# A GFNet and GEGLU kernel on one core: norm 0 earlier, four tiles per bank for slabs 0 and 1, first loads in one queue

## The chip, the cores and the metric

The kernel runs on one core of a Trainium2 chip. The metric is device time in microseconds (us), lower is better. Engines are named as in the profile: PE (TensorE matmul), PEld (its weight load), DVE (VectorE), ACT (ScalarE), POOL (GpSimd) and SP (SyncE, here only a queue of transfers).

## The reference

The input `x` is 2048 x 640 in bf16. It is normalised along its 640 columns to `xn`. Two branches read `xn`; the result is `x + s * g`.

```python
xn = layernorm(x)                                   # (x - mean) / sqrt(var + 1e-5)
X  = rfft2(xn) * (w_r + 1j * w_i)                   # 2048 x 321 spectrum
s  = irfft2(X)                                      # 2048 x 640
g  = silu((gelu_tanh(xn @ w_gate) * (xn @ w_up)) @ w_down)   # 640 -> 1536 -> 640
return x + s * g
```

## The kernel before

**Data.** The 2048 rows stand as 16 slabs of 128 rows; slab `n1` holds rows `16*n2 + n1`. `X` is the whole input on chip, 16 x 640 elements on each of 128 partitions, and is normalised in place. A group is four slabs. `xnT[g]` holds the transposed normalised slabs of group `g`, 640 rows (five chunks of 128) by 512 columns: it is the moving operand of the up and gate products. `Wg`, `Wu` and `Wd` are the weights; the 1536 hidden columns are 12 tiles of 128. `UT` holds the product of gate and up of one group, transposed.

**The feed-forward stage.** For one tile and one `k` (0 gate, 1 up), `ffn_piece` issues five matmuls that add up in a PSUM bank `psg` or `psu`, of which there are two each. Then ACT applies GELU to the gate bank and writes `ge` (L837), and DVE multiplies the up bank with `ge` into `UT` (L839). A bank is free again when its reader is done.

**Order.** Everything is issued in an order written out by hand. PE runs through the list `back`; after entry `s` of `back` the items that were `put` at slot `s` are issued. Each engine runs its own instructions in that order. Entries 0 to 15 are the first part of group 0: entry 0 is slab 0 against tiles 0 and 1 (128 columns), with the transposes of slab 1 in its middle; entry 1 is slab 1 against the same tiles; entries 2 to 7 are tiles 2 to 7 against slabs 0 and 1 (256 columns), 8 to 15 are tiles 0 to 7 against slabs 2 and 3. From entry 16 on a tile and `k` have an entry each with 512 columns; slot 24 begins the down projection of group 0. The Fourier stages (`slab_S1`, `slab_D`, `s2_step` and so on) are put between later entries.

**Before entry 0.** `warm_pe(21)` issues 21 matmuls of 256 columns on ones, so that PE is running while the first loads arrive. On DVE stand `stats(0)` (two `bn_stats` of 320 columns each and their `bn_aggr`) and both halves of slab 1's statistics. `root_act(0)` has ACT make 1/sqrt(var + eps) of slab 0, and then load the GELU table; `root` of slab 1 takes the way over DVE (`ve`) and POOL (`pow`). `norm_parts(0)` normalises columns 0 to 383 and then 384 to 639; `slab_Tparts(0)` transposes the five chunks on PE and evicts them in two parts, the first by DVE, the second by ACT.

**Loads.** SP's queue brings the slabs, `Wu` tiles 0 to 5 and all that follows; ACT's queue brings `Wg` tiles 0 to 5, two tiles at a time. At most eight transfers are outstanding: the ninth waits for the first to land.

**POOL's part.** Besides the roots, POOL makes integer tables by `iota`, then six one-column constants in `inv_rest` (from five that DVE makes in `inv_consts`), the phases `tinv_phase` (two halves of 128 x 1024), `ft_phase(0, k)` in three steps, and then, put at slot 13, `root(4, 4)` and `shift(4, 4)`, which give scale and bias (`rst`, `nmr`) for `norm_act` of slabs 4 to 7 on ACT, put at slots 15, 17, 19 and 21.

Of the kernel before, what the change touches and what calls it, by code (L numbers as in the profile page):

```python
# [76 lines left out]
def build(nc, env):  # L77
# [5 lines left out]
    def load_x(n0, n, eng=nc.sync):  # L83
        eng.dma_start(out=X[:, n0:n0 + n, :], in_=xv[:, n0:n0 + n, :])

    def load_w(k, t0, t1, eng=nc.sync):
        f0, f1 = t0 * P, t1 * P
        eng.dma_start(out=(Wg, Wu)[k][:, :, f0:f1], in_=(wgv, wuv)[k][:, :, f0:f1])

    def load_gu(t0, t1):  # L90
        for k in range(2):
            load_w(k, t0, t1)

    load_x(0, 1)
    load_x(1, 1)
    load_w(1, 0, 2)
    load_w(1, 2, 4)
    load_x(2, 1)
    load_w(1, 4, 6)
    load_x(3, 1)  # L100
    load_gu(6, 8)
    load_x(4, 4)
    load_gu(8, 12)
    load_x(8, 4)
# [68 lines left out]
    def c1(name, dt=FP32):  # L173
        return consts.tile([P, 1], dt, name=name)
# [35 lines left out]
            rstd[n0 + k] = r[:, k:k + 1]  # L210

    def root_act(n1):
        rstd[n1] = c1("rst0")
        nc.scalar.activation(out=rstd[n1], in_=mva[n1 // 4][:, n1 % 4, 1:2], func=ACT.Abs_reciprocal_sqrt, bias=eps)
        nc.scalar.activation(out=warm, in_=negpi, func=ACT.Gelu_apprx_tanh)

    def norm(n1, c0=0, c1_=D):
# [10 lines left out]
    eps = c1("eps")  # L228
    nc.vector.memset(eps, 1e-5)
    nc.scalar.activation(out=warm, in_=eps, func=ACT.Abs_reciprocal_sqrt)  # L230
    for t in (0, 2, 4):
        load_w(0, t, t + 2, nc.scalar)
    b_0, b_1 = c1("b_0"), c1("b_1")
    nc.vector.memset(b_0, 320.0)
    nc.vector.memset(b_1, 0.0)
# [583 lines left out]
    def bank(k):  # L819
        return psA.tile([P, 512], FP32, tag="gu"[k], name="ps" + "gu"[k])  # L820
# [17 lines left out]
        else:  # L838
            nc.vector.tensor_tensor(out=UT[:, t, c0:c1_], in0=ps, in1=ges[t], op=ALU.mult)  # L839

    def ffn_part(g, t, h):
        for k in range(2):
            ffn_piece(g, t, k, h * 256, h * 256 + 256)

    def ffn_half(g, t, k):
        ffn_piece(g, t, k, 0, 512)
# [122 lines left out]
            if t == NT - 1:  # L969
                gated(g, j, k, ph)  # L970

    def ffn_slab(j, tk):
        for t, k in tk:
            ffn_piece(0, t, k, j * P, j * P + P)

    GG, UU = ((0, 0), (1, 0)), ((0, 1), (1, 1))

    def run(*items):
        for it in items:
            it[0](*it[1:])  # L980
# [3 lines left out]
    def norm_parts(n1):  # L984
        for a, b in PARTS:
            norm(n1, a * P, b * P)

    def slab_Tparts(n1):
        if n1 == 0:
            xnT[0] = slot(0, 5, 512)  # L990
        for (a, b), ev in zip(PARTS, (nc.vector.tensor_copy, nc.scalar.copy)):
            pt = psB.tile([P, 5, P], BF16, tag="b")
            for c in range(a, b):
                nc.tensor.transpose(out=pt[:, c, :], in_=X[:, n1, c * P:(c + 1) * P], identity=ident)  # L994
            ev(out=xnT[0][:, a:b, n1 * P:n1 * P + P], in_=pt[:, a:b, :])
        done.add(("T", n1))

    NP = 8
    STR = (1, 2)
    back = [(run, (ffn_slab, 0, GG), (norm_parts, 1), (slab_Tparts, 1), (vt_iota, 1), (ffn_slab, 0, UU),  # L1000
             (inv_consts, 0), (inv_consts, 1)),
            (run, (ffn_slab, 1, GG + UU), (stats, 2), (root, 2, 1))]
    for h in range(2):
        for t in range(0 if h else 2, NP):
            back.append((ffn_part, 0, t, h))
        if h == 0:
            back[-1] = (run, (ffn_piece, 0, NP - 1, 0, 0, 256), (slab_Tparts, 3), (ffn_piece, 0, NP - 1, 1, 0, 256))
    for g in range(4):
        for t in range(NP if g == 0 else 0, NT):
            for k in range(2):  # L1010
# [10 lines left out]
    def put(s, *item):  # L1021
        plan[s].append(item)

    put(1, inv_rest)
    put(2, norm, 2)
    put(3, bn_half, 3, 0)
    put(4, bn_half, 3, 1)
    put(4, bn_join, 3)
    put(4, root, 3, 1)
    put(4, slab_T, 2, 1)  # L1030
    put(5, norm, 3)
    for g in range(5):
        put(3 + g, ft_v, g)
        put(8 + g, ft_v, 5 + g)
# [98 lines left out]
        for k in range(n):  # L1133
            put(min(d + 8 + k, LAST), finish, n0 + k)

    warm_pe(21)
    bn_half(1, 1)
    bn_join(1)
    root(1, 1)
    norm_parts(0)  # L1140
    slab_Tparts(0)
    warm_pe(2)

    put(5, phase_const)

# [35 lines left out]
```

## Time and profile before

| | us |
|---|---|
| median of 3 runs | 193.73 (193.61 to 193.73) |
| the profiled execution | 193.65 |
| its span, first to last instruction | 191.9 |
| outside the span | 1.75 |
| PE busy | 186.1 |
| DVE busy | 150.9 |
| ACT busy | 131.9 |
| POOL busy | 53.9 |
| first warming matmul starts | 1.18 |
| first matmul of the feed-forward stage starts | 6.84 |
| entry 8 of `back` starts on PE | 16.50 |
| entry 16 of `back` starts on PE | 25.24 |

Times in the timeline are counted from the first instruction. A row of the timeline gives start, length, engine, line, operation, output and input, count, and in brackets how long the engine had been idle and what ended that. Matmuls overlap: a row of five that shows 0.71 us is followed by the next row after 0.55. The share of a queue entry named "SPq" or "ACTq" is the issue of a transfer, not the transfer.

### The profile page before, as it was taken

How to read it: one execution, taken by the hardware profiler on the slowest of the kernel's cores; microseconds unless marked ns; L12 is line 12 of the kernel's file. 1: busy time of each engine (PE TensorE's matmuls, PEld its weight loads, DVE VectorE, ACT ScalarE, POOL GpSimd, SP SyncE). 2: the span in 40 equal slices, each digit the busy share in tenths (PEclk: the TensorE clock that was granted, in tenths of full speed). 3: DMA queues.
4: the chain of work that ended last, by engine and by line, in shares of the span. 5: the costliest groups of instructions: out<-in, count | busy, mean ns of one | idle time of the engine just before them, and what ended most of it. 6: DMA issues, size and time to landing. Idle time of an engine off the chain costs nothing.

```text
span 191.9 us, 4068 instructions
## 1 busy us (share of the span) xinstructions
PE 186.1 (97%) x1453; PEld 115.6 (60%) x1469; DVE 150.9 (79%) x364; ACT 131.9 (69%) x241; POOL 53.9 (28%) x91
## 2 busy tenths in 40 slices
PE   7999999999999999999999999999999999999993
PEld 5788854677655665566543334347775555556772
DVE  6787889899799889846978677685445898888973
ACT  4658557957878778536697878634989776876622
POOL 4458768999040200000000000002030134150400
PEclk9999999999999999999999999999999999999999
DMA  6999999948889994249996444149900084778842
GB/s 164 300 329 360 370 332 170 172 99 318 178 165 191 211 300 120 78 111 230 223 108 123 106 103 103 42 107 273 266 5 0 0 117 111 152 153 213 121 174 62
DMA packets 39700, 32.43 MB, mean 169 GB/s; under 512 B 12928, under 2 KB 37760, under 8 KB 39552
## 3 DMA queue, kind: packets, MB, share of 16 engines
q1 hardware_dynamic: 35888, 27.91, 58.6%
q0 software_dynamic: 1824, 3.28, 9.4%
q10 hardware_dynamic: 1968, 0.98, 1.9%
q8 instruction: 11, 0.18, 0.4%
q14 instruction: 9, 0.07, 0.1%
HBM read 19.03 MB, written 7.88 MB: 140 GB/s over the span
## 4 chain that ended last, share of the span: by engine, by line
PE 95%; DMA 2%; DVE 1%; issue 1%; SPq 0%; ACT 0%
PE psu L832 27%; PE psg L832 27%; PE psg L967 7%; PE psg L933 7%; PE psu L967 6%; PE psu L933 5%; PE pu L657 2%; PE pd L762 2%; PE pv L735 2%; PE pz L555 2%; PE pd L573 2%; PE px L628 2%; DMA X<-in_A_x_dram 2%; PE pt L994 1%; PE pd L575 1%
## 5 line engine op out<-in xcount | busy, mean ns | idle before, releaser
L832 PE MATMUL psu<-XG,Wu 128*128 128x512 bf16 (+2 forms) x284 | 60.4, 342 | 0.5 <-issue 0.3
L832 PE MATMUL psg<-XG,Wg 128*128 128x512 bf16 (+2 forms) x280 | 60.1, 341 | 0.6
L839 DVE TENSOR_TENSOR UT<-psu,ge 128x512 bf16<-128x512 f32 (+2 forms) x58 | 34.4, 594 | 13.6 <-PE psu L832 8.1
L837 ACT ACTIVATE ge<-psg 128x512 bf16<-128x512 f32 (+2 forms) x58 | 30.3, 523 | 21.3 <-PE psg L832 20.6
L832 PEld LDWEIGHTS <-Wu 128*128 128x128 bf16 x290 | 25.9, 98 | 20.9 <-issue 3.4
L832 PEld LDWEIGHTS <-Wg 128*128 128x128 bf16 x290 | 26.5, 98 | 18.8 <-issue 0.2
L967 PEld LDWEIGHTS <-UT 128*128 128x128 bf16 x204 | 19.1, 98 | 6.9
L813 POOL DMA_DIRECT2D VY<-in_A_x_dram x12 | 10.6, 964 | 26.2 <-ACT W L737 10.5
L713 POOL COPY vr<-VY 128x128 bf16<-128x128 bf16 x2 | 0.6, 291 | 60.2 <-DMA VY<-UDR 60.2
L644 DVE TENSOR_TENSOR RZ<-xs,W 128x960 bf16<-128x960 bf16 (+2 forms) x22 | 13.3, 647 | 4.4 <-ACT xs L640 4.4
L967 PE MATMUL psg<-Wd,UT 128*128 128x320 bf16 (+1 forms) x108 | 15.7, 290 | 0.0
L578 ACT CAST RZ<-pd 128x660 bf16<-128x660 f32 x16 | 11.3, 706 | 5.2 <-PE pd L575 5.2
L189 DVE BATCH_NORM_STATS2 st<-X 128x6 f32<-128x320 bf16 x32 | 14.0, 476 | 0.6 <-DMA X<-in_A_x_dram 0.4
L933 PEld LDWEIGHTS <-UT 128*128 128x128 bf16 x120 | 11.4, 98 | 4.8 <-issue 0.4
L967 PE MATMUL psu<-Wd,UT 128*128 128x320 bf16 (+1 forms) x96 | 13.9, 293 | 0.0
L737 ACT CAST W<-pv 128x640 bf16<-128x640 f32 x16 | 11.1, 691 | 3.1 <-PE pv L735 3.1
L763 ACT ACTIVATE W<-pd 128x640 bf16<-128x640 f32 x16 | 11.3, 706 | 1.5 <-PE pd L762 1.5
L557 ACT CAST GEN<-pz 128x640 bf16<-128x640 f32 x16 | 11.2, 698 | 1.2 <-PE pz L555 1.2
L672 ACT CAST RX<-pu 128x480 bf16<-128x480 f32 (+3 forms) x22 | 10.8, 489 | 1.1 <-DVE RX L672 0.3
L640 ACT CAST xs<-px 128x960 bf16<-128x960 f32 (+2 forms) x11 | 10.3, 933 | 0.0
L207 POOL TENSOR_TENSOR rst<-ve,mhalf 128x1 f32<-128x1 f32 (+1 forms) x6 | 5.5, 913 | 11.5 <-DVE ve L205 11.5
L933 PE MATMUL psg<-X,UT 128*128 128x320 bf16 x48 | 7.8, 300 | 0.0
(202 smaller groups left out, 302.1 us busy)
## 6 DMA issues: line engine op xcount, KB each, us to landing
ZDR<-RZ SPq DMA_DIRECT2D x16, 160.5 KB, 4.1
UDR<-RX SPq DMA_DIRECT2D x10, 240.8 KB, 3.1
B<-ZDR SPq DMA_DIRECT2D x8, 240.8 KB, 5.2
W<-UDR SPq DMA_DIRECT2D x2, 963.0 KB, 9.1
X<-in_A_x_dram SPq DMA_DIRECT2D x3, 640.0 KB, 10.3
Wd<-in_B_w_down_dram SPq DMA_DIRECT2D x1, 1920.0 KB, 14.6
VY<-in_A_x_dram POOLq DMA_DIRECT2D x12, 160.0 KB, 4.3
out_dram<-VY SPq DMA_DIRECT2D x12, 160.0 KB, 2.8
```

Source lines behind the costliest of these rows:

```text
L189: nc.vector.bn_stats(out=st_n[n1][:, k, :], in_=X[:, n1, 320 * k:320 * k + 320])
L557: nc.scalar.copy(out=Zt[n1], in_=pz)
L578: nc.scalar.copy(out=zd.rearrange("p c (q e) -> p c q e", e=10), in_=pd[:, :, 0:330].rearrange("p c (e q) -> p c q e", q=33))
L644: nc.vector.tensor_tensor(out=pp[-1], in0=xs, in1=WT[:, :, h0:h0 + n, l0:l0 + w], op=ALU.mult)
L672: copy(out=out, in_=src)
L737: nc.scalar.copy(out=vs, in_=pv)
L763: nc.scalar.activation(out=parts(eobuf, i, 5)[:, :, n1 - DG[i][0], :], in_=pd, func=ACT.Copy, scale=(2.0 if n1 // 4 in BY_SILU else 1.0) / ...
L832: nc.tensor.matmul(ps, lhsT=WT[:, c, t * P:(t + 1) * P], rhs=xnT[g][:, c, c0:c1_], start=(c == 0), stop=(c == 4))
L837: nc.scalar.activation(out=ges[t], in_=ps, func=ACT.Gelu_apprx_tanh)
L839: nc.vector.tensor_tensor(out=UT[:, t, c0:c1_], in0=ps, in1=ges[t], op=ALU.mult)
L933: nc.tensor.matmul(ps, lhsT=lhs[:, t, :], rhs=rhs[:, t, :], start=(t == 0 and i in (0, 1, 3)), stop=(t == 5), skip_group_check=i in (2, 4, ...
L967: nc.tensor.matmul(ph, lhsT=UT[:, t, j * P:(j + 1) * P], rhs=Wd[:, t, c0:c1_], start=(t == 0), stop=(t == NT - 1))
```

## The change

- The first loads stand in SP's queue alone: slab 0, slab 1, `Wg` tiles 0 to 3 in one piece (640 KB), `Wu` tiles 0 and 1, `Wu` tiles 2 and 3, slab 2, `Wg` tiles 4 to 7 in one piece, slab 3, `Wu` tiles 4 to 7 in one piece, and then as before. A row of a four-tile piece is 1024 bytes, of a two-tile piece 512.
- `norm_parts(0)` and the transposes of slab 0 stand behind the first half of slab 1's statistics; the second half, and slab 1's root, now on ACT like slab 0's, follow them. The GELU table is loaded behind both roots. Both parts of slab 0's and of slab 1's transposes are evicted by DVE. 19 warming matmuls stand ahead of the transposes and 4 behind (21 and 2 before).
- A new `ffn_multi` puts several tiles in one bank: slabs 0 and 1 alone against tiles 0 to 3 (four tiles of 128 columns in a bank), then tiles 4 to 7 against both, and tiles 0 to 7 against slabs 2 and 3, two tiles of 256 columns to a bank. GELU and product then take a bank of 512 columns in one instruction. Entries 0 to 15 are sixteen as before, each of the same number of columns as before; entry 6 has the transposes of slab 2 in its middle, entry 7 those of slab 3.
- Statistics, roots and norms of slabs 2 and 3 are put at slots 1 to 5; `inv_consts` and `inv_rest` are put at slot 7, ahead of `tinv_phase`.

```diff
     load_x(0, 1)
     load_x(1, 1)
+    load_w(0, 0, 4)
     load_w(1, 0, 2)
     load_w(1, 2, 4)
     load_x(2, 1)
-    load_w(1, 4, 6)
+    load_w(0, 4, 8)
     load_x(3, 1)
-    load_gu(6, 8)
+    load_w(1, 4, 8)
     load_x(4, 4)
...
     def root_act(n1):
-        rstd[n1] = c1("rst0")
+        rstd[n1] = c1("rst%d" % n1)
         nc.scalar.activation(out=rstd[n1], in_=mva[n1 // 4][:, n1 % 4, 1:2], func=ACT.Abs_reciprocal_sqrt, bias=eps)
+
+    def gelu_table():
         nc.scalar.activation(out=warm, in_=negpi, func=ACT.Gelu_apprx_tanh)
...
-    for t in (0, 2, 4):
-        load_w(0, t, t + 2, nc.scalar)
...
+    def ffn_multi(k, t0, n, c0, c1_, half=None):
+        w = c1_ - c0
...
+        if half in (None, 0):
+            cur["m"] = bank(k)[:, 0:n * w].rearrange("p (t w) -> p t w", w=w)
+        ps = cur["m"]
+        WT = (Wg, Wu)[k]
+        for i in range(n) if half is None else range(half * n // 2, (half + 1) * n // 2):
+            for c in range(5):
+                nc.tensor.matmul(ps[:, i, :], lhsT=WT[:, c, (t0 + i) * P:(t0 + i + 1) * P], rhs=xnT[0][:, c, c0:c1_],
+                                 start=(c == 0), stop=(c == 4))
+        if half == 0:
+            return
+        flush()
+        if k == 0:
+            ge = work.tile([P, 512], BF16, tag="ge", bufs=3, name="ge")[:, 0:n * w].rearrange("p (t w) -> p t w", w=w)
+            ges[t0, c0] = ge
+            nc.scalar.activation(out=ge, in_=ps, func=ACT.Gelu_apprx_tanh)
+        else:
+            nc.vector.tensor_tensor(out=UT[:, t0:t0 + n, c0:c1_], in0=ps, in1=ges[t0, c0], op=ALU.mult)
...
-        for (a, b), ev in zip(PARTS, (nc.vector.tensor_copy, nc.scalar.copy)):
+        for (a, b), ev in zip(PARTS, (nc.vector.tensor_copy, nc.scalar.copy if n1 > 1 else nc.vector.tensor_copy)):
...
-    back = [(run, (ffn_slab, 0, GG), (norm_parts, 1), (slab_Tparts, 1), (vt_iota, 1), (ffn_slab, 0, UU),
-             (inv_consts, 0), (inv_consts, 1)),
-            (run, (ffn_slab, 1, GG + UU), (stats, 2), (root, 2, 1))]
-    for h in range(2):
-        for t in range(0 if h else 2, NP):
-            back.append((ffn_part, 0, t, h))
-        if h == 0:
-            back[-1] = (run, (ffn_piece, 0, NP - 1, 0, 0, 256), (slab_Tparts, 3), (ffn_piece, 0, NP - 1, 1, 0, 256))
+    back = [(run, (ffn_multi, 0, 0, 4, 0, P), (vt_iota, 1)),
+            (run, (ffn_multi, 1, 0, 4, 0, P, 0), (slab_Tparts, 1), (ffn_multi, 1, 0, 4, 0, P, 1)),
+            (run, (ffn_multi, 0, 0, 4, P, 256)),
+            (run, (ffn_multi, 1, 0, 4, P, 256))]
+    for h, k, t0 in ((0, 0, 4), (0, 0, 6), (0, 1, 4), (0, 1, 6)) + tuple((1, k, t) for t in (0, 2, 4, 6) for k in range(2)):
+        back.append((ffn_multi, k, t0, 2, 256 * h, 256 * h + 256))
+    back[6] = (run, (ffn_multi, 1, 4, 2, 0, 256, 0), (slab_T, 2, 1), (ffn_multi, 1, 4, 2, 0, 256, 1))
+    back[7] = (run, (ffn_multi, 1, 6, 2, 0, 256, 0), (slab_Tparts, 3), (ffn_multi, 1, 6, 2, 0, 256, 1))
...
-    put(1, inv_rest)
-    put(2, norm, 2)
-    put(3, bn_half, 3, 0)
-    put(4, bn_half, 3, 1)
-    put(4, bn_join, 3)
-    put(4, root, 3, 1)
-    put(4, slab_T, 2, 1)
-    put(5, norm, 3)
+    put(1, stats, 2)
+    put(1, root, 2, 1)
+    put(2, bn_half, 3, 0)
+    put(2, bn_half, 3, 1)
+    put(3, norm, 2)
+    put(3, bn_join, 3)
+    put(3, root, 3, 1)
+    put(5, norm_parts, 3)
+    for part in range(2):
+        put(7, inv_consts, part)
+    put(7, inv_rest)
...
-    warm_pe(21)
+    warm_pe(19)
+    norm_parts(0)
+    slab_Tparts(0)
+    warm_pe(4)
     bn_half(1, 1)
     bn_join(1)
-    root(1, 1)
-    norm_parts(0)
-    slab_Tparts(0)
-    warm_pe(2)
+    root_act(1)
+    gelu_table()
+    norm_parts(1)
```

9 lines of the change are left out of this document (2 added, 7 removed).

## The prediction

> **What bounds the kernel now.** I read the page first, then the timeline of the first 35 us, then the transfers with their landings, then the waits of ACT and the timeline of POOL.
>
> ```profile
> span 191.9 us, 4068 instructions
> PE 186.1 (97%) x1453; PEld 115.6 (60%) x1469; DVE 150.9 (79%) x364; ACT 131.9 (69%) x241; POOL 53.9 (28%) x91
> ...
> PE 95%; DMA 2%; DVE 1%; issue 1%; SPq 0%; ACT 0%
> ```
>
> TensorE is the bound: 95% of the chain that ended last lies on it, and of 5.8 us without a matmul some 1.2 lie ahead of the first one and about 4 behind the last. A change can win only by letting the real matmuls begin earlier, and only if nothing stops them afterwards. When they begin, the timeline shows:
>
> ```profile
> 1.18 4.55 PE L588 MATMUL psg<-GEN 128*128 128x256 bf16 x21 [1.18 <-DVE eps L229]
> ...
> 4.05 0.21 DVE L195 BATCH_NORM_AGGREGATE mva<-st 128x2 f32<-128x12 f32 x1
> 4.29 0.29 ACT L214 ACTIVATE rst<-mva,eps 128x1 f32<-128x1 f32 x1 [2.08 <-DVE mva L195]
> 4.38 0.89 DVE L189 BATCH_NORM_STATS2 st<-X 128x6 f32<-128x320 bf16 x2
> 4.60 1.28 ACT L215 ACT_TABLE_LOAD   x1
> 5.30 0.21 DVE L195 BATCH_NORM_AGGREGATE mva<-st 128x2 f32<-128x12 f32 x1
> 5.55 0.15 DVE L205 TENSOR_SCALAR ve<-mva 128x1 f32<-128x1 f32 x1
> 5.62 0.63 DVE L218 TENSOR_SCALAR X<-X,mva,rst 128x384 bf16<-128x384 bf16 x2
> ...
> 6.05 0.54 PE L994 MATMUL pt<-ident,X 128*128 128x128 bf16 x5 [0.32 <-DVE X L218]
> ...
> 6.84 0.76 PE L832 MATMUL psg<-XG,Wg 128*128 128x128 bf16 x10
> ```
>
> The root of slab 0 is there at 4.58, but its norm starts at 5.62, behind the statistics of slab 1. That second is the prize. From 6.84 on no wait of PE is longer than 0.2 us until its last matmul, so any gain carries to the end unless a new wait eats it.
>
> **The start.** The new order puts norm 0 behind one half of slab 1's statistics. That half waits for slab 1's load, which landed at 4.38; a half takes 0.41 start to start, so norm 0 could start at 4.80 and the transposes 0.43 later (5.62 to 6.05 above), at 5.22. PE isn't free sooner: 19 warming matmuls at 0.213 end at 5.23. Should slab 1's load come earlier, that covers it; should it come later, each tenth costs a tenth. The old pace of 0.213 for 256 columns falls to 0.109 only with the 21st warming matmul at 5.4, so I take the transposes at double their 0.056: the third starts at 5.44, with 0.27 of latency the eviction starts at 5.71, takes 0.36, and 0.05 later (as in the trace) the first real matmul starts at 6.12. Both evictions now stand on DVE; the second (about 0.3) ends at 6.3, where the fourth matmul is at 6.29: a few hundredths, as ACT's eviction cost before. Gain: 6.84 - 6.12 = **0.72 us**.
>
> **Slab 1.** Its root goes from DVE plus POOL (0.65) to one ACT instruction of 0.29, ahead of the GELU table load (1.28 + 0.20). Statistics end about 6.95, root 7.27, norm 7.3 to 7.96; PE reaches the transposes at 6.12 + 0.06 + 20 x 0.0557 + 10 x 0.0557 = 7.85, so the wait is nil to 0.1. The table is ready about 8.8, and GELU of the first bank ends at 9.4. Nobody is late: the third user of that buffer pair starts at 10.9. Cover gone, each tenth beyond 10.9 costs a tenth.
>
> **Matmuls and evictions.** Before: 40 of 128 columns and 140 of 256; after: 80 and 120. The timeline gives 10 of 128 columns 0.56 us and 5 of 256 columns 0.55: nothing changes for PE. Evictions become fewer and wider: ACT 4 x 0.28 + 14 x 0.38 = 6.4 before, 8 x 0.58 = 4.6 after; DVE 4 x 0.29 + 14 x 0.42 = 7.0 before, 8 x 0.62 = 5.0 after. All of it lies beside PE: worth nothing by itself. DVE's chain GELU 0, product, statistics 2 and 3, product, norms 2 and 3 runs back to back from 9.4 and gets the transposes of slab 3 evicted by about 15.8, where PE wants them (6.12 + 9.7): a tie, with any lateness of PE as its cover.
>
> **The loads.** Landings, as issue plus time to landing:
>
> ```profile
> issues: line engine op xcount, KB each, median us to landing
> Wu<-in_B_w_up_dram SPq DMA_DIRECT2D x1, 320.0 KB, 6.7
> X<-in_A_x_dram SPq DMA_DIRECT2D x1, 160.0 KB, 6.8
> ```
>
> The first is Wu of tiles 2 and 3, issued at 2.15, so landed at 8.8, with 1600 KB issued up to it on both queues. The other pieces in the same way: 640 KB at 5.5 us, 1280 at 7.7, 2400 at 11.5, 3200 at 14.2: two queues gave one rate, about 290 KB/us. Pieces of tiles 8 to 11, with rows twice as long, landed at 18.8 and 20.7: 640 KB in 1.87 us against 2.2 for short rows, so 0.35 saved per large piece. In the new order Wg 0-3 is at 960 KB: 6.6 less 0.35 = 6.25, wanted at 6.12. Wu 2-3 is at 1600: 8.8 less 0.35 = 8.46, wanted at 8.13 (7.85 and five transposes). Wg 4-7 at 2400: 11.5 less 0.7 = 10.8, wanted at 10.9. Wu 4-7 at 3200: 14.2 less 1.05 = 13.15, wanted at 13.1. The largest lateness counts, not the sum: **loss 0.33**. Bounds: 0 if the early rate is a little higher, 1.1 (14.2 - 13.1) if large pieces come no faster. I take 0.33, nearest to the measured landings. Issuing is no limit: 14 issues at about 0.5 each, and the wait for one of eight outstanding transfers now falls on earlier ones.
>
> **What is moved to slot 7.** `inv_consts` and `inv_rest` leave slots 0 and 1 for slot 7, ahead of POOL's phase work. POOL before, on the timeline, and what ACT waited for from 6 to 40 us:
>
> ```profile
> 15.50 2.38 POOL L334 TENSOR_SCALAR GEN<-GEN,u,ph_t 128x1024 int32<-128x1024 int32 x2 [0.67 <-DVE ph_t L282]
> 17.85 0.74 POOL L370 TENSOR_SCALAR GEN<-GEN 128x660 f32<-128x660 f32 x1
> 18.68 2.45 POOL L372 TENSOR_SCALAR GEN<-GEN 128x660 f32<-128x660 f32 x1
> 21.21 1.49 POOL L374 TENSOR_TENSOR GEN<-GEN 128x660 f32<-128x660 f32 x1
> 25.27 1.04 POOL L207 TENSOR_TENSOR rst<-ve,mhalf 128x4 f32<-128x4 f32 x1 [2.57 <-DVE ve L205]
> ```
>
> ```profile
> ACT X L461 <- POOL nmr L456: 1.5, 1, 1.5
> ```
>
> POOL had 2.57 us to spare before the root of slabs 4 to 7. Let T be the end of slot 7 on PE (16.50 before). Afterwards the last product of slot 7 starts at T + 0.27, the constants follow at T + 0.9, and POOL starts `inv_rest` at T + 1.1. That takes 1.99 (11.84 to 13.83 before), the two phase instructions 2.35, the three of `ft_phase` 4.85 (17.85 to 22.70): T + 10.3. Root to `norm_act(4)` on ACT is 1.54 (25.27 to 26.81): T + 11.85, where it was 26.81 - 16.50 = T + 10.31. Queued behind `norm_act(4)` on ACT is the GELU of slot 16, whose bank slot 20 wants; it ended at 28.22, slot 20 started at 29.55: cover 1.33, used 1.54: **loss 0.21**. Behind that GELU waits DVE's product of slot 17, then that of slot 19, whose bank slot 23 wants: ended 31.52, wanted 32.79, cover 1.27, less 1.54, with 0.21 already given: **loss 0.06**. By slot 22 ACT has caught up (it stood 0.5 and 0.76 us waiting for PE at 30.8 and 33.0). Bounds: 0 if POOL's instructions run 3% shorter, 0.8 if 5% longer.
>
> **Sum.** -0.72 + 0.33 + 0.21 + 0.06 = -0.12. The profiled execution took 193.65, of which 191.9 is the span; the median of the runs is 193.73. 193.65 - 0.12 = 193.53; forecast **193.5**.
>
> **Rivals.** (1) The cover holds: loads and POOL come in time, PE keeps 0.5 to 0.72: 192.9 to 193.2. For: the loads are late only by tenths, and the stretches from 3.5 to 5.0 us moved 333 to 344 GB/s where those from 5.5 to 10 moved 291 to 313, so the first megabyte may come faster. Against: four deadlines in a row stand within 0.3 us. (2) Large pieces are no faster, and Wu 4-7 lands 1.1 after PE wants it: -0.72 + 1.1 + 0.27 = +0.65, 194.3. It turns the sign once that landing is later than 13.6. For: one queue must bring 3200 KB where two did; against: 640 KB in 1.87. (3) POOL's chain runs 5% longer and slots 20 and 23 wait 0.7 to 0.9: 194.0 to 194.2. (4) The clock: if the pace of 0.213 goes on beyond 6.12, real work runs at half speed. It changed 4.25 us after the first matmul; if the transposes at 5.23 began that count anew, it would change at 9.5 and lose (9.5 - 6.12) / 2 = 1.7: 195.2. For: 19 matmuls end at 5.23, before the change at 5.4. Against: the four warming matmuls follow after only 0.4 of transposes. The Trainium skill, "TensorE: Matmul & The Clock Gate", "What's actually happening", says the gate opens after a busy window of about 3.4 us that runs freely, and "Part 4: PE-mode transpose" that transposes do not count as busy in the same way: by that rule this could happen. The one trace, with its change 4.25 us on, neither refutes nor shows it. (5) Norm 0 still waits for slab 1's load, so the order changes less than it says: if that lands 0.3 later than 4.38 the gain is 0.4; near the forecast.
>
> **How the numbers follow.** 0.2% is 0.39 us, about what a measurement of this kernel can tell. Forecast with (5), 193.3 to 194.1: 0.48, likeliest range that one. Rival 1: 0.28. Rival 2: 0.12. Rival 3 at its upper end: 0.07. Rival 4: 0.05. So faster 0.28, same 0.48, slower 0.24. The range leaves out rival 4 and the ends of 1 and 2: 192.95 to 194.4.
>
> **What would show it.** First real matmul at 6.1 to 6.3 instead of 6.84; a PE wait for a Wu load near 8.2; POOL without a gap before the root at about T + 10.3; PE waiting for ACT at slot 20. No waits at all means rival 1; a wait near 13 us of about 1 means rival 2; matmuls of 128 columns at 0.107 means rival 4. Wrong altogether if PE loses time after slot 24.

## The result

The changed kernel takes 196.89 us (median of 6 runs, 195.75 to 197.58) against 193.85 for the kernel before (6 runs in the same session): a ratio of 1.0157, 95% interval 1.0135 to 1.0178. One of those six runs of the kernel before took 327.87 us; the median of the other five is 193.73. The change makes the kernel slower by 1.6%, and the time lies 2.5 us outside the predicted range. The profiled execution took 196.73 us. Its page:

```profile
span 194.4 us, 4065 instructions
PE 186.9 (96%) x1473; PEld 116.4 (60%) x1489; DVE 150.8 (78%) x356; ACT 130.3 (67%) x230; POOL 53.9 (28%) x90
...
PE 83%; POOL 6%; DMA 6%; issue 2%; SPq 1%; DVE 1%; ACT 0%; ACTq 0%; DVEq 0%; POOLq 0%
```

TensorE's work has hardly changed (186.1 busy before, 186.9 now). What has changed is the chain: PE carried 95% of it, now 83%, and POOL and DMA have 6% each. So something stops TensorE. The timeline of the changed kernel shows the first places:

```profile
4.27 0.30 ACT L215 ACTIVATE rst<-mva,eps 128x1 f32<-128x1 f32 x1 [2.05 <-DVE mva L196]
4.60 0.63 DVE L221 TENSOR_SCALAR X<-X,mva,rst 128x384 bf16<-128x384 bf16 x2
5.20 0.74 PE L1007 MATMUL pt<-ident,X 128*128 128x128 bf16 x5
5.77 0.56 DVE L1008 COPY XG<-pt 128x384 bf16<-128x384 bf16 x2 [0.53 <-PE pt L1007]
7.32 1.29 PE L852 MATMUL psg<-XG,Wg 128*128 128x128 bf16 x20 [0.60 <-DMA Wg<-in_B_w_gate_dram]
9.51 0.56 PEld L852 LDWEIGHTS <-Wu 128*128 128x128 bf16 x10 [0.24 <-DMA Wu<-in_B_w_up_dram]
```

Norm 0 now starts at 4.60, where it started at 5.62 before. The evictions are done at 6.33, but the first real matmul starts at 7.32, and was at 6.84 before: it waits for Wg of tiles 0 to 3. At 9.52 it has stopped again, for Wu of tiles 2 and 3 (landed at 9.47), and lost 0.24 more. The next place is further on, in three views of the timeline (POOL, VectorE, then ACT and PE):

```profile
20.41 2.39 POOL L335 TENSOR_SCALAR GEN<-GEN,u,ph_t 128x1024 int32<-128x1024 int32 x2
23.60 2.98 POOL L373 TENSOR_SCALAR GEN<-GEN 128x660 f32<-128x660 f32 x1
26.66 1.82 POOL L375 TENSOR_TENSOR GEN<-GEN 128x660 f32<-128x660 f32 x1
28.45 1.03 POOL L208 TENSOR_TENSOR rst<-ve,mhalf 128x4 f32<-128x4 f32 x1
23.53 0.76 DVE L340 TENSOR_SCALAR GEN<-GEN,andm,orm 128x1024 int32<-128x1024 int32 x1
26.04 1.10 DVE L340 TENSOR_SCALAR GEN<-GEN,andm,orm 128x1024 int32<-128x1024 int32 x1
29.98 0.92 ACT L462 ACTIVATE X<-X,nmr,rst 128x640 bf16<-128x640 bf16 x1 [4.29 <-POOL nmr L457]
31.43 1.24 PE L833 MATMUL psg<-XG,Wg 128*128 128x512 bf16 x5 [0.98 <-ACT ge L838]
```

POOL stands without a gap before the root (28.45), as forecast, but two instructions of `ft_phase` are longer than before: 2.98 and 1.82 against 2.45 and 1.49. ACT waits 4.29 us for POOL's root, and TensorE 0.98 at slot 20.

Laying the two traces side by side, slot 16 starts 0.74 late (0.48 from the first stop, 0.24 from the second), slot 20 1.88, and after slot 23 the lag is 1.96. At 133 us, where a load into `VY` comes later, it grows to 2.39, and TensorE's last matmul ends 2.34 late (190.99 against 188.66). The work behind it is 0.20 longer. That makes the span. The execution as a whole is 2.32 us longer than its span where it was 1.78 before, another 0.54: 2.34 + 0.20 + 0.54 = 3.08, the difference of 196.73 and 193.65. In the other five runs of the changed kernel the time beyond the span was 2.15 to 3.58.

So there are four things to explain: the start, slot 20, the transfer at 133 us, and the time beyond the span.

### The profile page after: what moved, and what is told of

It is laid out like the page before. It is cut to its first block, busy times and chain, and to the rows that moved or that the text cites. A ratio compares the mean times of both kernels' runs of the same rounds, so it can differ in the third digit from the quotient of the medians.

```text
span 194.4 us, 4065 instructions
## 1 busy us (share of the span) xinstructions
PE 186.9 (96%) x1473; PEld 116.4 (60%) x1489; DVE 150.8 (78%) x356; ACT 130.3 (67%) x230; POOL 53.9 (28%) x90
## 3 DMA queue, kind: packets, MB, share of 16 engines
HBM read 19.03 MB, written 7.88 MB: 138 GB/s over the span
## 4 chain that ended last, share of the span: by engine, by line
PE 83%; POOL 6%; DMA 6%; issue 2%; SPq 1%; DVE 1%; ACT 0%; ACTq 0%; DVEq 0%; POOLq 0%
PE psg L833 21%; PE psu L833 21%; PE psg L986 7%; PE psu L986 6%; PE psg L952 5%; PE psu L952 5%; DMA Wu<-in_B_w_up_dram 3%; PE pu L658 2%; PE pd L763 2%; PE pz L556 2%; DMA VY<-UDR 2%; PE pv L736 2%; PE psu L852 2%; PE pd L574 2%; PE px L629 2%; PE psg L852 2%
## 5 line engine op out<-in xcount | busy, mean ns | idle before, releaser
L833 PE MATMUL psg<-XG,Wg 128*128 128x512 bf16 x190 | 48.7, 379 | 1.5 <-ACT ge L838 1.0
L833 PE MATMUL psu<-XG,Wu 128*128 128x512 bf16 x194 | 49.0, 379 | 0.5 <-issue 0.3
L840 DVE TENSOR_TENSOR UT<-psu,ge 128x512 bf16<-128x512 f32 x40 | 27.4, 687 | 12.0 <-PE psu L833 6.1
L838 ACT ACTIVATE ge<-psg 128x512 bf16<-128x512 f32 x40 | 23.9, 598 | 13.7 <-PE psg L833 12.9
L833 PEld LDWEIGHTS <-Wu 128*128 128x128 bf16 x200 | 17.9, 98 | 20.2 <-issue 3.6
L833 PEld LDWEIGHTS <-Wg 128*128 128x128 bf16 x200 | 18.5, 98 | 19.0 <-issue 1.3
L738 ACT CAST W<-pv 128x640 bf16<-128x640 f32 x16 | 11.1, 692 | 3.1 <-PE pv L736 3.1
L558 ACT CAST GEN<-pz 128x640 bf16<-128x640 f32 x16 | 11.1, 696 | 1.2 <-PE pz L556 1.2
L673 ACT CAST RX<-pu 128x480 bf16<-128x480 f32 (+3 forms) x22 | 10.8, 490 | 1.3 <-DVE RX L673 0.3
L852 PE MATMUL psg<-XG,Wg 128*128 128x256 bf16 (+1 forms) x100 | 9.9, 251 | 0.6 <-DMA Wg<-in_B_w_gate_dram 0.6
L852 PE MATMUL psu<-XG,Wu 128*128 128x256 bf16 (+1 forms) x100 | 10.4, 251 | 0.1
```

Of the source, the lines that this page charges most:

```text
L558: nc.scalar.copy(out=Zt[n1], in_=pz)
L738: nc.scalar.copy(out=vs, in_=pv)
L833: nc.tensor.matmul(ps, lhsT=WT[:, c, t * P:(t + 1) * P], rhs=xnT[g][:, c, c0:c1_], start=(c == 0), stop=(c == 4))
L838: nc.scalar.activation(out=ges[t], in_=ps, func=ACT.Gelu_apprx_tanh)
L852: nc.tensor.matmul(ps[:, i, :], lhsT=WT[:, c, (t0 + i) * P:(t0 + i + 1) * P], rhs=xnT[0][:, c, c0:c1_], start=(c == 0), stop=(c == 4))
```

## The experiments

All were timed in five rounds against the kernel before, whose median lay between 193.55 and 193.69 in these sessions. "Lag" is how much later TensorE does the same work than in the profiled run of the kernel before (negative: ahead). The table puts the profiled runs side by side; the last column is over all runs of a kernel.

| kernel | ratio to before | lag at slot 16 | behind slot 23 | at TensorE's end | beyond the span |
|---|---|---|---|---|---|
| before | 1 | 0 | 0 | 0 | 1.7 to 1.8 |
| changed | 1.0157 | 0.74 | 1.96 | 2.34 | 2.15 to 3.58 |
| old_loads | 1.0137 | 0.82 | 2.03 | 2.04 | 2.3 to 2.5 |
| inv_early | 1.0122 | 2.80 | 2.80 | 2.80 | 1.9 to 3.3 |
| both | 1.0102 | 1.80 | 1.80 | 2.16 | 1.8 to 3.8 |
| small_1q | 1.0137 | 0.26 | 1.47 | 1.84 | 2.4 to 2.5 |
| mask_late | 1.0164 | 1.04 | 1.84 | 2.44 | 2.5 to 3.9 |
| pad | 1.0134 | 0.50 | 1.72 | 2.17 | 1.7 to 1.8 |
| small_inv | 1.0117 | 0.93 | 0.93 | 0.94 | 1.9 to 4.2 |
| small_inv_pad | 1.0085 | 1.01 | 1.01 | 1.45 | 1.7 to 3.3 |
| norm0_alone | 1.0001 | -0.05 | -0.05 | -0.05 | 1.7 to 1.8 |
| norm0_1q | 1.0013 | 0.75 | 0.75 | 0.75 | 1.8 |
| regroup_alone | 1.0075 | 0.52 | 0.52 | 0.53 | 1.8 to 2.4 |
| norm0_root | 1.0001 | 0.01 | 0.01 | 0.01 | 1.7 to 1.8 |
| norm0_evict | 0.9999 | -0.31 | -0.31 | -0.30 | 1.7 to 1.9 |
| pairs | 1.0056 | 0.74 | 0.74 | 1.34 | 2.0 to 2.1 |
| pairs_pad | 1.0038 | 0.84 | 0.84 | 0.99 | 1.8 |

From slot 16 to slot 23 the lag grows by 1.2 in every kernel with the constants in slot 7 (0.8 in mask_late), and not at all in any with the constants in slots 0 and 1.

**1. The old loads.** The first loads as before, on two queues in pieces of two tiles; all else as changed.

```
-    load_w(0, 0, 4)  ...  load_w(0, 4, 8)  ...  load_w(1, 4, 8)
+    load_w(1, 4, 6)  ...  load_gu(6, 8)
+    for t in (0, 2, 4):
+        load_w(0, t, t + 2, nc.scalar)
```

> The changed kernel with the loads of before (Wg tiles 0 to 5 two at a time in ACT's queue, the rest two at a time in SP's). Theory A (two separate losses: loads about 1.0 us late, POOL's chain about 1.1): first real matmul at 6.2 to 6.4 instead of 7.32, no wait for a load, PE's wait at slot 20 stays at about 1.0; span 194.4 less 1.0 to 1.3, about 193.2. Rival B (one cause: the late start of PE is what lets POOL's chain collide): the wait at slot 20 falls below 0.3 too and the span comes to about 192.2. Rival C (the gain of the early norm is lost elsewhere, the clock changes at 6.4): first matmuls of 128 columns at 0.107 apart until the change, start early but no gain over 0.5.

**2. The old place of the constants.** `inv_consts` and `inv_rest` back in slots 0 and 1, all else as changed.

```
+            ... (vt_iota, 1), (inv_consts, 0), (inv_consts, 1)),
+    put(1, inv_rest)
-    for part in range(2):
-        put(7, inv_consts, part)
-    put(7, inv_rest)
```

> The changed kernel with inv_consts and inv_rest in slots 0 and 1 again. Theory A: the root of slabs 4 to 7 no longer waits for POOL, ACT's norm of slab 4 starts near 27.5, the wait of 0.98 at slot 20 and the 0.08 at slot 23 are gone: 1.05 less, span about 193.3; first real matmul stays at about 7.3. Rival B: the start is as late as before and the chain collides all the same; the wait at slot 20 stays over 0.5, span 194 or more.

**3. Both together.**

> Both taken back: the loads of before and the constants in slots 0 and 1; the early norm and the wide banks stay. Theory A: the losses add, 2.0 to 2.3 less than the changed kernel's span of 194.4, about 192.2, and if the early norm is worth what was forecast (0.6 to 0.7) below the 191.9 of before, 191.2 to 191.6. Rival B: no more than the better of the two alone (193.2). Rival D (the rest of the change, wide banks and early norm, loses by itself): span above 192.3 with no wait of PE at slot 20 and none for a load.

**4. Small pieces, one queue.** Pieces of two tiles in the order of the changed kernel.

```
-    load_w(0, 0, 4)
+    load_w(0, 0, 2)
+    load_w(0, 2, 4)
```

(and so for the two pieces of tiles 4 to 7).

> The changed kernel with every weight piece cut to two tiles, all still in SP's queue and in the same order. Theory E (size: a piece counts only when its last engine is done, and a large one hides that half of it is long there): Wg tiles 0 and 1 land near 5.6, first real matmul at 6.2 to 6.6, but Wu tiles 2 and 3 still land at 9 to 9.5 and PE waits there; span about 0.3 lower or the same. Theory F (one queue: two of the sixteen engines run about 1 us behind whatever the size): first real matmul at 6.6 or later, Wu 2-3 at 9.5, span the same within 0.2. If the short rows are slower too (512 bytes instead of 1024), Wu 2-3 lands after 9.8 and the span rises by 0.3.

Measured: the old loads 196.33 us (ratio 1.0137, 1.0116 to 1.0158), early constants 195.91 (1.0122, 1.0083 to 1.0162), both 195.33 (1.0102, 1.0079 to 1.0126), small pieces 196.18 (1.0137, 1.0120 to 1.0153). Each takes something back, none much.

The early constants take the wait at slot 20 away: there is none in the runs of 2 and 3, and it stays at 1.0 in those of 1 and 4. They bring a smaller one of 0.32 at slot 8, shown under 7 and 8. The start is another matter. With the old loads TensorE starts sooner and then stops. The timeline of the kernel with both:

```profile
5.98 0.75 PE L853 MATMUL psg<-XG,Wg 128*128 128x128 bf16 x10
8.87 0.73 PE L853 MATMUL psg<-XG,Wg 128*128 128x128 bf16 x10 [2.14 <-DMA Wg<-in_B_w_gate_dram]
```

After ten matmuls it wants Wg of tiles 2 and 3, which landed at 8.82 here, at 8.15 in the run with the old loads alone, and at 7.73 in the kernel before, which first used them at 9.34. So undoing the loads alone cannot mend the start: the four tiles to a bank ask for these weights about 2.8 us earlier than the old grouping did. Small pieces in one queue come off best at the start (first matmul at 6.47, lag 0.26).

In the profiled run with early constants the start was lost in still another way:

```profile
7.69 2.31 PE L852 MATMUL psg<-XG,Wg 128*128 128x128 bf16 x20 [1.69 <-DVE x_e L273]
9.79 1.27 PE L852 MATMUL psu<-XG,Wu 128*128 128x128 bf16 x10
```

```profile
PEclk9789999999999999999999999999999999999999
```

The wait is booked to VectorE, but Wg 0-3 landed at 7.64, which released it. Twenty matmuls then take 2.31 us, where the changed kernel's line above has 1.29 for the same twenty, and the granted clock dips in the second and third slices. The warming matmuls had gone over to the fast pace by 4.32 in this run. After 1.69 us without a matmul the pace fell back to 0.107 for 128 columns, and it came back to 0.056 at 11.1, 3.4 us later; the granted clock between 7.7 and 11.1 is 0.50. Of the lag of 2.80 at slot 16, 0.85 is the late start, about 1.6 the slow pace and 0.32 slot 8. The Trainium skill, "TensorE: Matmul & The Clock Gate", "What's actually happening", describes a free-running window of about 3.4 us that decides the pace; the return 3.4 us later agrees with it. It speaks of one idle window before the clock falls; here 1.69 us were enough. Against a simple threshold stands the run with both, where a gap of 2.14 us left the fast pace as it was. Nor does the work before it decide: in the 3.4 us after the change to the fast pace PE was busy for 1.61 us here (4.3 to 7.7) and for 1.53 in the run with both (5.2 to 8.6), where no fall came. Where the gap lies in the window may matter; no run here shows it. It happened once: among the 116 timed runs of the changed kernel and its variants this is the only one with a mean granted clock under 0.997 (0.991).

**5. The masks later.** The changed kernel with VectorE's two `tinv_mask` in slot 16, behind POOL's `ft_phase`.

```
-    put(12, tinv_mask, 0)
-    put(14, tinv_mask, 1)
+    put(16, tinv_mask, 0)
+    put(16, tinv_mask, 1)
```

> The changed kernel with both calls of tinv_mask moved from slots 12 and 14 to slot 16, behind ft_phase. Theory (VectorE's integer masks slow POOL's ft_phase when they run beside it, 5.7 instead of 4.85 us): ft_phase falls back to about 4.85, norm_act(4) comes 0.8 earlier, PE's wait at slot 20 falls from 0.98 to about 0.2, and the time falls by 0.7 to 0.9, to about 196.0. Rival (POOL is slow there for another reason, or the chain is held by the constants before it): ft_phase stays near 5.7, the wait at slot 20 stays near 1.0, time as the changed kernel, 196.9.

Measured: 196.71 us (1.0164, 1.0135 to 1.0193), the time not lower. The timeline says more:

```profile
23.89 2.45 POOL L373 TENSOR_SCALAR GEN<-GEN 128x660 f32<-128x660 f32 x1
26.43 1.49 POOL L375 TENSOR_TENSOR GEN<-GEN 128x660 f32<-128x660 f32 x1
27.88 1.49 POOL L208 TENSOR_TENSOR rst<-ve,mhalf 128x4 f32<-128x4 f32 x1
27.16 2.04 DVE L340 TENSOR_SCALAR GEN<-GEN,andm,orm 128x1024 int32<-128x1024 int32 x2
31.32 1.02 PE L833 MATMUL psg<-XG,Wg 128*128 128x512 bf16 x4 [0.56 <-ACT ge L838]
```

`ft_phase` is back at 2.45 and 1.49, to the hundredth what it was before. Now the masks run beside the root instead, which takes 1.49 where it took 1.03. So that half of the theory holds, and TensorE's wait falls from 0.98 to 0.56, not to 0.2. But a mask does not slow every POOL instruction beside it. The root and the second mask, in the kernel with early constants and in the kernel before:

```profile
28.09 0.81 DVE L340 TENSOR_SCALAR GEN<-GEN,andm,orm 128x1024 int32<-128x1024 int32 x1
28.26 1.53 POOL L208 TENSOR_TENSOR rst<-ve,mhalf 128x4 f32<-128x4 f32 x1 [3.52 <-DVE ve L206]
```

```profile
25.45 0.81 DVE L339 TENSOR_SCALAR GEN<-GEN,andm,orm 128x1024 int32<-128x1024 int32 x1
```

With the mask 0.17 ahead the root takes 1.53. In the kernel before the root started first (25.27), and took 1.04 with the whole mask beside it. Wherever the two meet in the traces of this case it goes by that order: 1.49 to 1.53 in eight kernels with a mask ahead, 1.04 in five with the root ahead. The Trainium skill, "SBUF — State Buffer", "SBUF: two separate sides", says that VectorE and GpSimd share one pair of ports, and that for some VectorE instructions whichever starts first holds the pair to its end while the other is blocked; the order agrees. The amount does not quite: `ft_phase`'s second instruction, which started with 0.69 of the mask still to run, was 0.53 longer, not 0.69. The time did not fall since Wg 0-3 landed at 7.57 in the profiled run (7.27 in the changed kernel), which is 0.3 of the 0.4 gained, and since 2.5 to 3.9 us lay beyond the span.

**6. Padding.** The changed kernel with instructions whose results nobody uses.

```
+    for k in range(10):
         nc.scalar.activation(out=warm, in_=eps, func=ACT.Abs_reciprocal_sqrt)
+    def pad(a, d):
+        if a:
+            nc.scalar.copy(out=pad_t, in_=eps)
+        if d:
+            nc.vector.memset(pad_u, 0.0)
+    for k in range(10):
+        for r in range(3):
+            put(28 + 5 * k, pad, k < 8, r < 2)
```

> The changed kernel with instructions that do nothing useful: nine more tiny activations while ACT waits for the first load, 24 one-column copies on ACT and 20 one-column memsets on DVE, two or three in each of ten slots from 28 to 73. In the changed kernel the time beyond the span is 2.2 to 3.6 us, 1.75 before, and an 8 KB transfer of instructions lies behind the last instruction (at 196.6), where the kernel before has its last ones at 176 and 187. Theory (ACT and DVE have 23 and 18 instructions fewer, so that their last piece of code is fetched at the very end of the program, in the open): with the padding these transfers lie ahead of 192, and the time beyond the span is 1.75 to 1.85 in every run; time about 0.6 to 0.9 below the changed kernel, 196.1. Rival (the time beyond the span has another cause): it stays at 2.2 to 3.6, time 196.9 or a few tenths more for the work added.

Measured: 196.23 us (1.0134, 1.0119 to 1.0149). The time beyond the span is 1.74 to 1.81 in all four runs, as in the kernel before; in the changed kernel it was never under 2.15. The queue of instruction transfers has on the pages of the kernel before, the changed one and the padded one, in this order:

```profile
q14 instruction: 9, 0.07, 0.1%
```

```profile
q14 instruction: 7, 0.06, 0.1%
```

```profile
q14 instruction: 9, 0.07, 0.1%
```

In the transfer records of the traces, the kernel before has its last two at 176 and 187 us, the padded one at 180 and 189. The changed kernel has neither inside its span, and one of 8 KB at 196.6, 2.2 us behind its last instruction. In the kernel before the last piece for ACT is fetched with about 316 of its 334 instructions done, the last for VectorE with 447 of 459, each about 128 instructions after the one before it. The changed kernel has 311 and 441: it ends just short of both, so a fetch would fall into the end of the program. Which engine a fetch belongs to is read from this spacing; the records do not name it. That padding brings the time beyond the span down is shown; that the late fetch is what lengthens it is not. In the profiled runs of three kernels as short as the changed one (inv_early, both, small_inv) the records hold no fetch behind the last instruction, and 1.9, 2.1 and 3.2 us lie beyond the span all the same.

**7 and 8. Small pieces with early constants, without and with padding.** These are the edits of 2 and 4, and then 6 on top.

> The changed kernel with weight pieces of two tiles in the one queue and with inv_consts and inv_rest back in slots 0 and 1. Theory (two separate losses: late large pieces at the start, POOL's chain at slot 20): slot 16 starts within 0.3 of the kernel before, no wait at slots 20 and 23, PE's end 0.2 to 0.8 behind the kernel before (the transfer at 133 us is worth up to 0.5), span 192.2 to 192.9, time 194.3 to 195.0 with about 2.2 beyond the span. Rival (the work of POOL and DVE in slots 0 and 1 delays the norm of slab 1, or loads come late anyway): a wait of 1 us or more ahead of the tenth us, time 195.3 to 196.

> The same with the padding: small pieces, early constants, and the instructions that do nothing. Theory (the losses add up: loads 0.5, POOL 1.1, code at the end 0.6): span as small_inv, 192.2 to 192.9, 1.8 beyond it, 194.0 to 194.7, so 0.2 to 0.6% above the kernel before, less if the transfer at 133 us comes early. Rival (padding doesn't help): as small_inv.

Measured: 195.60 us (1.0117, 1.0072 to 1.0163) and 195.19 (1.0085, 1.0061 to 1.0109). No wait at slots 20 and 23. TensorE's end is 0.94 and 1.45 behind the kernel before, more than hoped. Wg 2-3 and Wu 0-1 were waited for 0.4 us each in the first: they landed at 7.13 and 8.26, where the run of experiment 4 had 6.76 and 7.88. A third wait stands at slot 8. VectorE's rows in the first of the two kernels, and a line of TensorE's waits:

```profile
16.43 0.69 DVE L865 TENSOR_TENSOR UT<-psu,ge 128x512 bf16<-128x512 f32 x1 [0.34 <-ACT XG L551]
17.04 0.35 DVE L1011 COPY XG<-pt 128x384 bf16<-128x384 bf16 x1
PE psg L855 <- DVE XG L1011: 0.2, 1, 0.2
```

VectorE holds back the product of slot 6 until ACT has evicted slab 2, as the profile books it, and so evicts slab 3 late; slot 8, which needs slab 3, starts 0.31 after its turn. The same 0.31 or 0.32 is lost in the runs of 2, 3 and 8 and with the grouping alone (experiment 11), in every kernel with four tiles to a bank and the constants in slots 0 and 1. With the constants in slot 7 the product starts before that eviction ends (16.14 against 16.27 in the changed kernel), and nothing is lost there. Why the early constants bring this wait was not settled. The padded kernel loses 0.44 more at 70 and 99 us, where the padded changed kernel loses the same, so the padding is not free. Beyond the span lie 1.9 to 4.2 us without padding, and 1.73 to 1.95 with it in five runs of six; the sixth had 3.27, which the padding does not explain. By their ratios the three repairs add up within the intervals: 0.35, 0.20 and 0.23% one by one, 0.72% together. What stays is in the start and at slot 8.

**9 to 11. The parts of the start, one by one, from the kernel before.** First norm 0 alone; then the same with the small pieces in one queue; then the grouping alone (four tiles to a bank, old loads, old constants, old order of the start). That last kernel still has the changed kernel's root of slab 1 on ACT, its evictions on VectorE and its slots for slabs 2 and 3. The edit of the first:

```
-    warm_pe(21)
+    warm_pe(19)
+    norm_parts(0)
     bn_half(1, 1)
     bn_join(1)
     root(1, 1)
-    norm_parts(0)
     slab_Tparts(0)
-    warm_pe(2)
+    warm_pe(4)
```

> The kernel before with one thing changed: norm 0 right behind its root, then the statistics and root of slab 1, then the transposes of slab 0; tiles per bank, loads and constants stay. In the trace of before the first use of a weight piece came behind its landing by 1.03 us (Wg 0-1), 0.62 (Wu 0-1), 1.61 (Wg 2-3), 1.00 (Wu 2-3), 0.10 and 0.47 (tiles 4 and 5), 0.78 and 0.26 (tiles 6 and 7). Theory (the loads stand just behind TensorE, so an earlier start finds the weights not there): first real matmul at 6.3 to 6.5, a wait for weights of tile 4 near 11.3, PE's end at most 0.1 to 0.2 earlier, time 193.4 to 193.7. Rival (the start is what binds, as the prediction's 0.72 supposed): PE keeps 0.4 to 0.5 to the end, time 193.1 to 193.2.

> As the kernel with norm 0 alone, and the weights of tiles 0 to 7 in pieces of two tiles in the one SyncE queue, gate and up in turn. In the kernel with small pieces in one queue they landed, in that order, at 5.6, 6.8, 7.9, 9.0 for tiles 0 to 3, 10.6 and 11.7 for 4 and 5, 13.3 and 14.2 for 6 and 7. Theory (one queue brings them in the order of need): the least slack against the uses of the kernel before is about 0.25 instead of 0.10, so PE ends 0.2 to 0.3 earlier, time 193.3 to 193.5. Rival (one queue comes late as a whole): a wait of 0.3 or more for a weight piece, time 193.8 to 194.3.

> The kernel before with the new grouping (four tiles of slabs 0 and 1 to a bank, then two tiles to a bank), and with the old loads, the old place of the constants and the old start (norm 0 behind slab 1's statistics). Theory (four tiles at once want Wg 2-3 half a microsecond after Wg 0-1, where the old grouping wanted it 2.8 us later): first real matmul near 6.84, a stop of 0.4 to 1.4 behind ten matmuls, until Wg 2-3 has landed at 7.7 to 8.8; slot 8 and all behind it 0.5 to 1.5 late, and 0.2 to 2 more beyond the span, since the program is shorter there too: time 194.4 to 196. Rival (the grouping is neutral, as the prediction had it): no such wait, time 193.6 to 193.9.

Measured: norm 0 alone 193.65 us (1.0001, 0.9993 to 1.0010), no difference. TensorE starts at 6.47, 0.37 ahead; the lead is 0.11 at slab 1's transposes, which wait for slab 1's norm, and 0.05 at the end. No weight was waited for, so the theory gave the right time and the wrong reason. With one queue 193.99 (1.0013, 1.0001 to 1.0025): the lead of 0.53 and then 0.26 is lost to Wu of tiles 4 to 7,

```profile
PEld L830 <- DMA Wu<-in_B_w_up_dram: 1.2, 2, 0.9
```

which landed at 12.03 for tiles 4 and 5 and at 15.28 for 6 and 7. In the run of experiment 4 the pieces in the same places of the queue (there Wg 6-7 and Wu 6-7) landed at 11.70 and 14.24. The spans of its twelve runs go from 191.7 to 192.9. The grouping alone costs 0.75% (194.95 us; 1.0075, 1.0051 to 1.0099): TensorE's end is 0.53 late, and 1.76 to 2.43 lie beyond the span. The stop for Wg 2-3 was short here (0.15), as they landed at 7.50. The first matmul started 0.23 earlier than before; the slow pace, which lasted to 7.1, cost about 0.25, and slot 8 the 0.31 of experiment 7. So only the 0.15 comes from the order in which the weights are wanted.

**12 and 13. Slab 1's root on ACT, then its second eviction on VectorE too.** The start of experiment 9 with the changed kernel's `root_act(1)` and `gelu_table()`, from the kernel before; both evictions of slab 0 stand on VectorE too.

```
-    root(1, 1)
     slab_Tparts(0)
+    root_act(1)
+    gelu_table()
```

> The kernel before with norm 0 right behind its root, both evictions of slab 0 on VectorE, and the root of slab 1 as one activation ahead of the GELU table, so that the norm of slab 1 no longer waits for POOL (in the kernel with norm 0 alone PE's start of 6.47, 0.37 ahead, shrank to 0.11 at slab 1's transposes, which waited for that norm). Theory (two things stand close behind the start, slab 1's norm and the weights of tiles 4 to 7, which landed at 11.35 to 14.12 in that kernel and were wanted at 11.42 to 14.43): the lead at slab 1's transposes grows to 0.3 to 0.4, a wait of 0.1 to 0.3 for weights of tile 4 or 6 takes most of it back, PE ends 0.1 to 0.2 earlier than the kernel before, time 193.45 to 193.6. Rival (only slab 1's norm held it): the lead of 0.3 to 0.4 lasts to the end, time 193.2 to 193.3.

> As the kernel with norm 0 early and slab 1's root on ACT, with slab 1's second eviction on VectorE too. There the lead of 0.36 us lasted to slab 1's transposes and was lost right behind them, since that eviction stood on ACT behind the GELU table and two GELUs (8.03). Theory A (ACT's queue took it): the lead lasts past 8.4; then theory B (the weights stand close behind: landed 11.2 to 11.6 for tiles 4 and 5, wanted at 11.47 and 12.03 without the lead) has PE wait 0.1 to 0.3 at tile 4, and the end is 0.1 to 0.2 earlier: time 193.4 to 193.6. If B is wrong, the whole 0.36 lasts: 193.25 to 193.35. If A is wrong, no lead behind 8.4: 193.6 to 193.7.

Measured: 193.64 us (1.0001, 0.9987 to 1.0014) and 193.59 (0.9999, 0.9984 to 1.0014). In the first the lead of 0.36 lasts to slab 1's transposes and is gone a microsecond later: its eviction stands on ACT behind the GELU table and two GELUs.

```profile
8.03 0.37 ACT L997 COPY XG<-pt 128x256 bf16<-128x256 bf16 x1
8.03 0.98 PE L834 MATMUL psg<-XG,Wg 128*128 128x128 bf16 x10
```

Neither the theory nor its rival had this; the weights were again in time. With that eviction on VectorE TensorE keeps 0.30 to its last matmul (188.36 against 188.66), and again no weight was waited for, so theory B falls: the profiled run took 193.34. Twelve runs spread over 193.34 to 194.24, and the ratio shows no difference. 0.3 us of 193.7 is 0.15%, less than this measurement tells.

**14 and 15. Pairs everywhere, without and with padding.** Two tiles to a bank for slabs 0 and 1 too, the old loads, the early constants, slab 1's statistics ahead of slab 0's evictions.

```
-    back = [(run, (ffn_multi, 0, 0, 4, 0, P), (vt_iota, 1)),
-            (run, (ffn_multi, 1, 0, 4, 0, P, 0), (slab_Tparts, 1), (ffn_multi, 1, 0, 4, 0, P, 1)),
-            ...
+    back = [(run, (ffn_multi, 0, 0, 2, 0, P), (slab_Tparts, 1), (vt_iota, 1), (ffn_multi, 1, 0, 2, 0, P),
+             (inv_consts, 0), (inv_consts, 1)),
+            (run, (ffn_multi, 0, 0, 2, P, 256), (ffn_multi, 1, 0, 2, P, 256))]
```

> The changed kernel's two tiles to a PSUM bank taken for slabs 0 and 1 too (two tiles where it has four), with the old loads, the constants in slots 0 and 1, and slab 1's statistics ahead of slab 0's evictions. Weights are wanted at 6.5 (Wg 0-1), 7.3 (Wu 0-1), 9.0, 10.1, 11.2, 12.3, 13.4 and 14.5 for the pairs behind them, and landed at 5.4, 7.0, 8.0, 8.7, 11.4, 11.3, 13.0 and 14.1 in the kernel with slab 1's root on ACT. Theory (four tiles at once was what the loads could not follow): no weight wait over 0.2 at the start, PE ends 0.1 to 0.4 earlier than the kernel before, span 191.5 to 191.8, and 0.2 to 1 more beyond the span than before since ACT and VectorE have fewer instructions: time 193.5 to 194.5. Rival (two tiles at once are late as well): waits of 0.4 or more, span 192.2 or more.

> The same with 24 one-column copies on ACT and 20 one-column memsets on VectorE in ten slots from 28 to 73. Theory (code at the end): 1.75 to 1.85 beyond the span in every run, time 193.2 to 193.6, level with the kernel before or 0.1 to 0.2% below it. Rival: as the kernel without them.

Measured: 195.02 us (1.0056, 1.0034 to 1.0078) and 194.46 (1.0038, 1.0022 to 1.0054). The first matmul starts at 6.14 and the lead of 0.7 holds for two slots. Then, of the waits of PE in the kernel without padding:

```profile
PE pt L545 <- DVE X L220: 0.6, 1, 0.6
PE psg L853 <- DMA Wg<-in_B_w_gate_dram: 0.4, 1, 0.4
```

Weights of tiles 4 and 5 came at 11.50, and the transposes of slab 2 started at 13.95, 0.75 late: their norm is behind on VectorE. So four tiles at once are not the whole of it: the regrouping loses even in pairs, through other waits. Padding again brings the time beyond the span from 1.98 to 2.14 down to 1.78 to 1.83 in every run. No version beat the kernel before.

## Why the prediction was wrong, step by step

The sum of -0.12 had two parts: the start with its loads, -0.72 + 0.33 = -0.39, and slots 20 and 23, +0.27. Measured in the profiled runs, the first is +0.74 and the second +1.22. Three terms were not in the sum at all: 0.38 at 133 us, 0.20 behind the last matmul and 0.54 beyond the span. Together that is 3.08.

- **Norm 0 earlier: the times right, the worth wrong.** Norm 0 was forecast for 4.80 and started at 4.60, since slab 1's load landed at 3.54; transposes 5.22, measured 5.20; eviction 5.71, measured 5.77. But "any gain carries to the end unless a new wait eats it" was taken as a gain of 0.72 to be kept. (Of the 5.8 us without a matmul, 3.2 and not about 4 lie behind the last one.) Done alone, in three forms, the step is worth 0.05, nothing and 0.30 us at TensorE's end, and nothing that the ratios can tell. Slab 1's norm and ACT's queue stand a few tenths behind the start, and TensorE's waits in the trace of before could not show that: they showed no wait, and not how little was missing to one.
- **The loads, +0.33: the term that failed first.** Forecast and landing: Wg 0-3 6.25 and 7.27, Wu 2-3 8.46 and 9.47, Wg 4-7 10.8 and 11.80, Wu 4-7 13.15 and 14.11. From piece to piece the forecast was right within 0.05; the whole row is 1.0 late, and so is its first member. A load is landed when the last of its 16 parts has come. Fourteen parts of Wg 0-3 were there at 6.11; the other two came at 7.08 and 7.27, and two stayed 1 us behind in every later piece. Three other kernels with this piece had it at 7.00, 7.57 and 7.64, with 11 or 12 parts there by 6.2 to 6.5. The estimate was taken from whole landings of small pieces and made shorter for the long rows; experiment 4, with small pieces, had the same bytes at 6.76. Why some parts lag is open.
- **"Nothing changes for PE" in the regrouping: true of its own time, and the wrong question.** The order in which weights are wanted changed. The grouping alone cost 0.53 at TensorE's end, of which 0.31 is slot 8, and stops of 1.6 and 2.1 us for Wg 2-3 appear in experiments 1 and 3. Together with the loads the start was forecast 0.39 early (0.72 less 0.33) and was 0.74 late at slot 16.
- **Slot 7, +0.21: right in kind, one instruction wrong in size.** The constants, `inv_rest` and the phase instructions came as forecast (POOL starts `inv_rest` at T + 1.15 for a forecast of T + 1.1, with T = 17.24). Then `ft_phase` took 5.68 instead of 4.85, since moving it later put it beside VectorE's masks, and `norm_act(4)` came at T + 12.74 for T + 11.85. 0.21 and the 0.83 make 1.04; the wait was 0.98, and the lag grew by 1.14. Slot 23 was forecast 0.06 and was 0.08. What an instruction meets at its new time was not asked; "0.8 if 5% longer" fell short of the 1.22. Early constants take this loss away and bring the 0.31 of slot 8 (experiments 2, 3, 7), so about 0.9 is what the move cost. The prediction had called the evictions of slab 3 a tie; in the changed kernel they were in time, at 17.15 for slot 8 at 17.24.
- **After slot 24, nothing: wrong by about 0.4.** The prediction itself named this as the sign that it would be wrong altogether. The lag at 133 us came with a load into `VY` that landed later. Among the 16 profiled runs it shows in five (0.41 to 0.64 in both, small_1q, mask_late, pairs and the changed kernel), and in none of the others. In these five the slower of the two pieces took 4.4 to 4.8 us from issue to landing, in all others 3.7 to 4.2. What makes it slow was not settled.
- **Beyond the span, unchanged: wrong by 0.5 and more.** The sum took this time over as it was. With fewer instructions it was longer, and padding with instructions that do nothing mends it in three kernels; that a late fetch of code is the reason is likely and not shown.
- **The rivals and the range.** Rival 2 put Wu 4-7 at 14.2 (landed 14.11) and rival 3 the wait at 0.7 to 0.9 (0.98). Both happened at once. They were priced as alternatives, and the range took the larger; by their own numbers the two together give -0.72 + 1.1 + 0.8 = +1.18, about 194.8. The rest of the way to 196.9 is the time beyond the span, the transfer at 133 us, the work behind the last matmul and the first piece. Rival 4 did not cost anything in the changed kernel: the transposes ran at the slow pace as forecast and the fast pace came only after 6.37, but the weights came later still. In the run with early constants the slow pace from 7.69 to 11.07 did cost about 1.6 us (by the two paces, 0.107 and 0.056), close to the 1.7 at which that rival was priced.

## What to carry to other kernels

When a start is moved earlier, list for every input of the next ten microseconds when it lands and when it is first used; the smallest difference, not the largest wait, bounds the gain, and bounds of independent steps are added, not chosen among. Before an instruction is moved on one engine, look at what the engine next to it runs at the new time, and take its duration from a row with the same neighbour. Keep an eye on the time between the span and the measured time: when a kernel becomes shorter in instructions and longer there, pad it with instructions that do nothing, and look at where its last fetches of code fall.

## What was not expected of the hardware

- Read from the records of the kernel before, ACT and VectorE each do about 128 instructions between their last two fetches of code. In the kernels that end a few instructions ahead of the last fetch, mostly 1.8 to 2.6 us lie beyond the span instead of 1.7 to 1.8, and in some runs 3 to 4; what adds either is open. With padding it was 1.73 to 1.95 in 17 of 18 runs.
- A POOL instruction of 2.45 us took 2.98, and one of 1.04 took 1.49 to 1.53, when one of VectorE's integer masks was already running as it started. When POOL's root started first, by 0.18 us, neither was longer than 1.04 and 0.81. A mask that started beside the 2.98 took 1.10.
- TensorE's pace went back to half after 1.69 us without matmuls in one run, for 3.4 us, and stayed full after 2.14 us in another. The first change to the fast pace came between 3.8 us (the padded kernel) and 7.1 us (the grouping alone) in different kernels with the same first matmul at 1.18.
- The 16 parts of one load can land 1.7 us apart (Wg 0-3 of the changed kernel: 5.57 to 7.27), the last two of them 1.0 and 1.2 us after the other fourteen.
